# One excursion per pair of heads instead of two, with the values in the MLP's free banks

## The chip, the cores and the metric

The kernel runs on one core of one Trainium2 chip. The metric is the device time of one execution in microseconds (us), given as the median of several executions. The kernel before took 1018.84 us (four runs, 1018.21 to 1020.08). The engines are TensorE (PE in the profile; PEld is its weight load), VectorE (DVE), ScalarE (ACT), GpSimd (POOL) and SyncE (SP), which issues the DMAs here.

## The reference

A retention block feeds an MLP. There are 8 batches, 8 heads, 576 positions and 64 values per head, all in float32.

```python
scores = scale * np.matmul(q, k.transpose(0, 1, 3, 2))
Dmat = np.where(rel >= 0, gamma[:, None, None] ** rel[None, :, :], 0.0)
attn_out = np.matmul(scores * Dmat, v)              # per batch and head
x = attn_out.transpose(0, 2, 1, 3).reshape(B * S, H * D)   # 4608 x 512
h = x @ w_in                                        # 512 x 2048
g = np.maximum(h, 0.0) + alpha * np.minimum(h, 0.0)
out = g @ w_out                                     # 2048 x 512
```

## The kernel before

**Retention.** A head's 576 positions are cut into 9 chunks of 64. Because the decay is a power of the distance, everything before a chunk can be folded into a 64x64 running sum of k-times-v products. So a chunk needs three things: its own 64x64 scores, the running sum of the chunks before it, and the product of both with v and q (the "values"). Two heads are worked on together as a pair; there are 8 x 4 = 32 pairs, numbered n. For one pair TensorE does 18 score products (L614), 16 state products k-times-v (L620) and 18 value products (L656). In the trace each product shows as two MATMUL records.

**MLP.** The 4608 tokens are cut into 18 blocks of 256, numbered kb. The hidden width of 2048 is cut into 8 units, numbered i, and one unit is the work of `mlp_unit(kb, i)`: 14 products of x with w_in (L463, the tiles `ph`), a chain of 11 instructions on VectorE and one on ScalarE that forms `g` (L471 to L487), and 7 products of `g` with w_out (L381, the tiles `po`). It uses 7 products for 2x2 blocks instead of 8. The w_out products are put off by one unit (`pend`), so TensorE's order is ph(u), po(u-1), ph(u+1), po(u), and so on, where u counts units.

**PSUM banks.** There are eight. The MLP's `ph` has two (tags `psh0` and `psh1`, pool `ps_h`), its `po` has four (`ps_o`), and the retention has two (tag `psa`, pool `ps_a`), which take scores, states and values in turn.

**Three phases.** Batches 0 and 1 and the preparation of the weights are written in a fixed order by hand. From batch 2 on (about 160 us into the run, loop `for b in range(2, B)`) the tile framework's scheduler orders the instructions of each engine from the program below. It inserts the waits between engines. MLP units of the blocks that are ready stand in `queue`, and the four pairs of batch b are strewn among them, 16 or 24 units a batch. After the last batch 24 units remain with no retention among them.

**A pair in that loop.** At the unit `u` where the pair begins, `pair_front` puts the scores and states between ph(u) and po(u-1). The 18 score products do not fit with the states into two banks, so the two of the ninth chunk go into a free quarter of the unit's own bank, `ph[0][:, 3]`; the code calls it `extra`. VectorE multiplies the scores by mask and decay into `mt` (L625 for the ninth chunk, L636 for the rest), and ScalarE copies the queries beside them (L632). `running_sums` and `pair_sums` (L583 to L597) run after unit u+1. After unit u+2 come the scaling and transposing of the next pair (`scale_pair`, L528 and L533; `transposes`, L539) and `pair_values`: the 18 value products between po(u+1) and ph(u+3), which ScalarE copies into the tokens' tiles `xb` (L665). So TensorE leaves the MLP twice for each pair. The loads of the next pair's k, q and v are issued by SP (L97, L105) into buffers two deep; a v buffer comes free when the value products of the pair before last are done.

Of the kernel before, what the change touches and what calls it, by code (L numbers as in the profile page):

```python
# [18 lines left out]
def kernel(  # L19
# [49 lines left out]
    def half(x):  # L69
        return slice(x * C, (x + 1) * C)  # L70
# [377 lines left out]
                          (t[:, 2], b21, t[:, 1])):  # L448
            nc.gpsimd.tensor_tensor(out=o, in0=x0, in1=x1, op=ALU.subtract)  # L449

    def mlp_unit(kb, i, front=None):
        if kb not in xt:
            combine_x(kb)
        x, t = xb[kb], xt[kb]
        ph = [ps_h.tile([P, 4, P], FP32, tag=f"psh{m}", name=f"ph{m}_{kb}_{i}")
              for m in range(2)]

        for n, (m, o, l, r) in enumerate((
                (0, 2, 0, x[:, 0:2, 0:P]), (0, 0, 2, x[:, 2:4, 0:P]), (0, 1, 5, t[:, 1]),
                (1, 0, 4, t[:, 0]), (1, 1, 1, x[:, 0:2, P:TB]),  # L460
                (1, 2, 6, x[:, 2:4, P:TB]), (1, 3, 3, t[:, 2]))):
            for cc in range(2):
                nc.tensor.matmul(ph[m][:, o], w_in[i // UST][:, l, i % UST, cc], r[:, cc],  # L463
                                 start=(n in (0, 3) and cc == 0), stop=(n in (2, 6) and cc == 1),
                                 skip_group_check=True)

        rest = front(ph[0][:, 3]) if front else None


        g = mlp.tile([P, 8, P], FP32, tag="g", name=f"g_{kb}_{i}")  # L470
        nc.scalar.copy(g[:, 7], ph[0][:, 2])  # L471
        for o, x0, x1 in ((g[:, 0:5:4], ph[0][:, 0:2], g[:, 7:8].to_broadcast([P, 2, P])),
                          (g[:, 5:7], ph[1][:, 0:2], g[:, 4:5].to_broadcast([P, 2, P])),
                          (g[:, 3], ph[1][:, 0], g[:, 6]),
                          (g[:, 1:3], ph[1][:, 2:4], g[:, 5:7])):
            nc.vector.tensor_tensor(out=o, in0=x0, in1=x1, op=ALU.add)  # L476
        for m in range(2):
            fc = m * NU + i
            nc.vector.tensor_scalar(g[:, 4 + 2 * m:6 + 2 * m], g[:, 2 * m:2 * m + 2], 0.0,  # L479
                                    alpha[:, fc:fc + 1], ALU.min, ALU.mult)  # L480
        nc.vector.scalar_tensor_tensor(  # L481
            out=g[:, 0:4].rearrange("p x t -> p (x t)"),
            in0=g[:, 0:4].rearrange("p x t -> p (x t)"), scalar=0.0,
            in1=g[:, 4:8].rearrange("p x t -> p (x t)"), op0=ALU.max, op1=ALU.add)
        for o, x0, x1, op in ((4, 1, 3, ALU.add), (6, 0, 1, ALU.subtract),
                              (5, 4, 0, ALU.subtract), (7, 2, 5, ALU.subtract)):
            ins = nc.vector.tensor_tensor(out=g[:, o, :], in0=g[:, x0, :], in1=g[:, x1, :], op=op)  # L487

        combine(3, ins)
        assert i < NU - UST or not waiting  # L490
        if rest:
            rest()
        pend.append((kb, i, g))
        if len(pend) > 1:
            mlp_out()
# [11 lines left out]
            if ready[kb] == b:  # L507
                queue.extend((kb, i) for i in range(NU))

    def pop_units(n, front=None):  # L510
        for _ in range(min(n, len(queue))):
            kb, i = queue.pop(0)
            mlp_unit(kb, i, front)
            if i == NU // 2 and kb + 1 < NKB and ready[kb + 1] <= done[0]:
                combine_x(kb + 1)

# [4 lines left out]
    def ps_tile(shape, name):  # L521
        return ps_a.tile(shape, FP32, tag="psa", name=name)
# [19 lines left out]
    def chunk(j):  # L542
        return slice(j * C, (j + 1) * C)
# [51 lines left out]
    def pair_sums(vn, su):  # L595
        for h2 in range(2):
            nc.scalar.copy(vn[half(h2), h2, 1:], su[half(h2)])  # L597
# [2 lines left out]

    later = []

    def pair_front(n, kT, qT, kn, vn):
        c = pairs[n][1]
        mts[n] = mt = attn.tile([P, 2 * S], FP32, tag="at", name=f"mt_{n}").rearrange(
            "p (h j s) -> p h j s", h=2, s=C)
        assert C == D and NJ == 9

        def products(extra):
            ps = [ps_tile([P, 2, NM - 1, C], f"ps{p2}_{n}") for p2 in range(2)]  # L610
            for j in (NJ - 1, *range(NJ - 1)):
                for h2 in range(2):
                    x = half((1 - h2, h2)[j % 2])
                    nc.tensor.matmul(extra[x, 0:C] if j == NJ - 1 else ps[j % 2][x, 0, j // 2],  # L614
                                     kT[half(h2), chunk(j)], qT[half(h2), chunk(j)],
                                     start=True, stop=True, skip_group_check=True)
            for j in range(NJ - 1):
                for h2 in range(2):
                    x = half((h2, 1 - h2)[j % 2])
                    nc.tensor.matmul(ps[j % 2][x, 1, j // 2], kn[half(1 - h2), j],  # L620
                                     vn[half(1 - h2), h2, j], start=True, stop=True,
                                     skip_group_check=True)
            for h2 in range(2):
                to = half(1 - h2)
                nc.vector.scalar_tensor_tensor(  # L625
                    out=mt[to, h2, NJ - 1], in0=extra[to, 0:C],
                    scalar=th[to, 3, 2 * c + h2:2 * c + h2 + 1], in1=mask[to],
                    op0=ALU.mult, op1=ALU.mult)

            def rest():  # L630
                for h2 in range(2):
                    nc.scalar.copy(mt[half(h2), h2].rearrange("p j s -> p (j s)"), qT[half(h2)])  # L632
                for p2 in range(2):
                    for h2 in range(2):
                        h, to, x = 2 * c + h2, half(1 - h2), (1 - h2, h2)[p2]
                        nc.vector.scalar_tensor_tensor(  # L636
                            out=mt[to, h2, p2:NJ - 1:2], in0=ps[p2][half(x), 0],
                            scalar=th[to, 3, h:h + 1],
                            in1=mask[to, None, :].to_broadcast([C, NM - 1, C]),
                            op0=ALU.mult, op1=ALU.mult)  # L640
                later.append(lambda: pair_sums(vn, running_sums(n, ps[0][:, 1], ps[1][:, 1])))

            return rest

        return products

    def pair_values(n, vn, mt):
        b, c = pairs[n]
        w = TB // C

        j1 = -b * NJ % w or w
        j1 += w if NJ - j1 > 6 else 0
        pv = [ps_tile([P, (j1, NJ - j1)[i], C], f"pv{i}_{n}") for i in range(2)]
        for j in range(NJ):
            for h2 in range(2):
                nc.tensor.matmul(pv[j >= j1][half(h2), j - (j1 if j >= j1 else 0)],  # L656
                                 vn[:, h2, j], mt[:, h2, j], start=True, stop=True)
        j = 0
        while j < NJ:
            kb, o = divmod(b * NJ + j, w)  # L660
            if kb not in xb:
                xb[kb] = ring.tile([P, NCC, TB], FP32, tag=f"x{kb % NRING}", name=f"xb_{kb}")
            m, i = min(w - o, NJ - j), j >= j1
            j0 = j - (j1 if i else 0)
            nc.scalar.copy(xb[kb][:, c, o * C:(o + m) * C].rearrange("p (j s) -> p j s", s=C),  # L665
                           pv[i][:, j0:j0 + m])
            j += m
# [276 lines left out]
    enqueue(0)  # L944
    enqueue(1)

    for b in range(2, B):


        nq, first, at = len(queue), b * NPAIR, {}  # L950
        for c in range(NPAIR):
            u = c * nq // NPAIR
            while queue[u][1] in (0, NU - 1):
                u += 1
            assert u + 2 < nq and (not at or at[c - 1] + 2 < u)
            at[c] = u
        begin = {u: first + c for c, u in at.items()}
        for u in range(nq):
            front = None
            if u in begin:  # L960
                n = begin[u]
                if n + 1 < len(pairs) and n + 1 not in loaded:
                    loaded[n + 1] = load_pair(n + 1)
                front = pair_front(n, *turned.pop(n), loaded[n][0], loaded[n][3])
            pop_units(1, front)
            if u - 1 in begin:
                later.pop(0)()
            if u - 2 in begin:
                n = begin[u - 2]
                if n + 1 < len(pairs):  # L970
                    scale_pair(n + 1)
                    turned[n + 1] = transposes(n + 1)
                pair_values(n, loaded[n][3], mts.pop(n))
                del loaded[n]
        enqueue(b)
    pop_units(len(queue))
    while pend:
        mlp_out()
# [28 lines left out]
```

## Time and profile before

| | |
|---|---|
| median of four runs | 1018.84 us |
| the profiled execution's own time | 1019.2 us |
| its span, first to last instruction | 1017.5 us |
| TensorE busy | 1000.9 us (98%) |
| VectorE busy | 775.6 us (76%) |
| ScalarE busy | 269.8 us (27%) |
| GpSimd busy | 178.7 us (18%) |
| granted TensorE clock over the span | 0.995 |

The page lists busy time by engine, the chain of work that ended last, and groups of instructions by source line. A row of a group reads: line, engine, operation, output <- inputs, shape, count, then busy time and mean duration in ns, then the idle time of that engine just before and what ended it. A row of the timeline reads: start in us, length in us, engine, line, operation, output <- inputs, shape, count, and in square brackets an idle time before it with what ended that. Ends of matmuls are modelled, so distances between starts are used here for TensorE.

### The profile page before, as it was taken

The numbers are of one execution on the slowest core, as the hardware profiler recorded it, in microseconds if no ns is written. First come the engines' busy times: TensorE is split into PE (matmuls) and PEld (weight loads), VectorE is DVE, ScalarE is ACT, GpSimd is POOL, SyncE is SP. The second block draws the span as 40 slices with busy tenths as digits, with TensorE's granted clock in tenths as the row PEclk, the third lists the DMA queues.
The fourth block names the chain that finished last, engine by engine and source line by source line (L and its number), as shares of the span: only waits on it lengthen the run. The fifth ranks groups of instructions, "written<-read, shape, count | busy, mean of one in ns | idle before, by whom it ended". The sixth has DMA issues, their size and how long they took to land.

```text
span 1017.5 us, 23084 instructions
## 1 busy us (share of the span) xinstructions
PE 1000.9 (98%) x9385; PEld 894.1 (88%) x9385; DVE 775.6 (76%) x2086; ACT 269.8 (27%) x605; POOL 178.7 (18%) x201
## 2 busy tenths in 40 slices
PE   6999999999999999999999999999999999999997
PEld 5666668899999999999999999999999999999997
DVE  6769967878787888768778788887878777667665
ACT  4656652223222222122021312232222211000000
POOL 5656674300200020100010000200010001010000
PEclk8999999999999999999999999999999999999999
DMA  9975744322231313112112313222313000000000
GB/s 241 245 185 151 181 75 95 61 59 49 60 57 44 65 30 69 28 42 48 44 25 57 60 45 60 57 48 59 58 45 60 13 23 1 22 1 21 2 21 22
DMA packets 229307, 64.30 MB, mean 63 GB/s; under 512 B 214336, under 2 KB 222544, under 8 KB 229200
## 3 DMA queue, kind: packets, MB, share of 16 engines
q1 hardware_dynamic: 227088, 62.29, 26.9%
q8 instruction: 74, 1.21, 0.5%
q10 hardware_dynamic: 2112, 0.53, 0.3%
q14 instruction: 33, 0.27, 0.1%
HBM read 53.35 MB, written 9.44 MB: 62 GB/s over the span
## 4 chain that ended last, share of the span: by engine, by line
PE 95%; DVE 3%; DMA 1%; ACT 1%; issue 0%; SPq 0%; DVEq 0%; ACTq 0%
PE ph L463 38%; PE po L381 37%; PE ph L419 6%; PE po L398 6%; PE pv L656 3%; PE ps L614 1%; PE ps L620 1%; DMA w_out<-in_k_dram 1%; PE ph L614 1%; DVE su L589 0%; DVE g L476 0%; PE pt L697 0%; DVE mt L636 0%; PE pv L775 0%; PE ps L556 0%
## 5 line engine op out<-in xcount | busy, mean ns | idle before, releaser
L381 PE MATMUL po<-w_out,g 128*128 128x256 f32 x1792 | 411.0, 381 | 0.2
L381 PEld LDWEIGHTS po<-w_out,g 128*128 128x128 f32 x1792 | 330.2, 190 | 42.7 <-DVE g L487 1.4
L476 DVE TENSOR_TENSOR g<-ph,g 128x256 f32<-128x256 f32 (+1 forms) x512 | 186.6, 385 | 129.2 <-ACT g L471 77.1
L463 PE MATMUL ph<-xb,w_in 128*128 128x128 f32 x2048 | 272.7, 276 | 0.0
L463 PEld LDWEIGHTS ph<-xb,w_in 128*128 128x128 f32 x2048 | 257.1, 192 | 7.8 <-issue 0.7
L463 PE MATMUL ph<-xt,w_in 128*128 128x128 f32 x1536 | 213.8, 275 | 0.7 <-DVE g L476 0.7
L463 PEld LDWEIGHTS ph<-xt,w_in 128*128 128x128 f32 x1536 | 192.2, 192 | 1.0 <-PE ph L463 0.8
L487 DVE TENSOR_TENSOR g<-g 128x128 f32<-128x128 f32 x512 | 126.2, 287 | 5.4
L471 ACT COPY g<-ph 128x128 f32<-128x128 f32 x128 | 34.2, 267 | 328.3 <-PE ph L463 219.8
L528 POOL TENSOR_TENSOR qx<-qx,tabx 128x576 f32<-128x576 f32 x28 | 32.1, 1147 | 377.9 <-DVE g L476 256.8
L481 DVE SCALAR_TENSOR_TENSOR g<-g 128x512 f32<-128x512 f32 x128 | 91.3, 713 | 3.8
L479 DVE TENSOR_SCALAR g<-g,alpha 128x256 f32<-128x256 f32 x256 | 84.2, 370 | 2.9
L597 ACT COPY vn<-su 64x512 f32<-64x512 f32 x56 | 34.6, 618 | 134.0 <-DVE su L591 133.3
L419 PE MATMUL ph<-xb,w_in 128*128 128x256 f32 x256 | 61.5, 396 | 0.7 <-ACT xb L783 0.7
L398 PE MATMUL po<-w_out,g 128*128 128x512 f32 x128 | 58.6, 599 | 0.9 <-DVE g L435 0.9
L419 PEld LDWEIGHTS ph<-xb,w_in 128*128 128x128 f32 x256 | 49.9, 198 | 10.9 <-issue 2.4
L625 DVE SCALAR_TENSOR_TENSOR mt<-ph,th,mask 64x64 f32<-64x64 f32 x48 | 13.6, 283 | 53.2 <-PE ph L614 52.8
L665 ACT COPY xb<-pv 128x256 f32<-128x256 f32 (+3 forms) x84 | 22.7, 323 | 111.1 <-PE pv L656 111.0
L636 DVE SCALAR_TENSOR_TENSOR mt<-ps,th,mask 64x256 f32<-64x256 f32 x96 | 46.1, 480 | 2.4
L533 ACT ACTIVATE vn<-vn,tabv 64x576 f32<-64x576 f32 x56 | 43.4, 775 | 8.1 <-DMA vn<-in_v_dram 7.0
L398 PEld LDWEIGHTS po<-w_out,g 128*128 128x128 f32 x128 | 23.4, 190 | 24.5 <-issue 21.8
L449 POOL TENSOR_TENSOR xt<-xb 128x256 f32<-128x256 f32 x16 | 11.6, 727 | 188.5 <-PE ph L463 188.5
(134 smaller groups left out, 746.6 us busy)
## 6 DMA issues: line engine op xcount, KB each, us to landing
out_dram<-osb SPq DMA_DIRECT2D x36, 256.0 KB, 2.3
kx<-in_k_dram SPq DMA_DIRECT2D x112, 72.0 KB, 2.4
qx<-in_q_dram SPq DMA_DIRECT2D x112, 72.0 KB, 2.9
vn<-in_v_dram SPq DMA_DIRECT2D x56, 144.0 KB, 3.0
kn<-in_k_dram SPq DMA_DIRECT2D x56, 144.0 KB, 3.3
raw<-in_moe_w_in_dram SPq DMA_DIRECT2D x24, 256.0 KB, 4.0
raw<-in_moe_w_out_dram SPq DMA_DIRECT2D x10, 512.0 KB, 4.2
w_in<-in_moe_w_out_dram SPq DMA_DIRECT2D x6, 512.0 KB, 5.6
```

What stands on the lines that cost most here:

```text
L381: nc.tensor.matmul(acc[kb][n // 2][:, n % 2, :], g[:, x, :], w_out[i][:, y, :], start=(i == 0 and n % 2 == 0), stop=(i == NU - 1 and (n % ...
L398: nc.tensor.matmul(acc[kb][m], g[:, 2 * x + m], w_out[i][:, 2 * x:2 * x + 2].rearrange("p x f -> p (x f)"), start=(i == 0 and x == 0), sto ...
L419: nc.tensor.matmul(ph[:, x], w_in[i // UST][:, cc // 2 * 2 + x, i % UST, cc % 2], xb[kb][:, cc], start=(cc == 0 and x == 0), stop=(cc == N ...
L463: nc.tensor.matmul(ph[m][:, o], w_in[i // UST][:, l, i % UST, cc], r[:, cc], start=(n in (0, 3) and cc == 0), stop=(n in (2, 6) and cc == ...
L471: nc.scalar.copy(g[:, 7], ph[0][:, 2])
L476: nc.vector.tensor_tensor(out=o, in0=x0, in1=x1, op=ALU.add)
L479: nc.vector.tensor_scalar(g[:, 4 + 2 * m:6 + 2 * m], g[:, 2 * m:2 * m + 2], 0.0, alpha[:, fc:fc + 1], ALU.min, ALU.mult)
L481: nc.vector.scalar_tensor_tensor(out=g[:, 0:4].rearrange("p x t -> p (x t)"), in0=g[:, 0:4].rearrange("p x t -> p (x t)"), scalar=0.0, in1 ...
L487: ins = nc.vector.tensor_tensor(out=g[:, o, :], in0=g[:, x0, :], in1=g[:, x1, :], op=op)
L533: nc.scalar.activation(vn[x, h2], vn[x, h2], ACTF.Copy, scale=tabv[x, c:c + 1])
L597: nc.scalar.copy(vn[half(h2), h2, 1:], su[half(h2)])
L636: nc.vector.scalar_tensor_tensor(out=mt[to, h2, p2:NJ - 1:2], in0=ps[p2][half(x), 0], scalar=th[to, 3, h:h + 1], in1=mask[to, None, :].to_ ...
```

## The change

The value products of pair n-1 and the scores and states of pair n are now issued together, in a function `joint(n)`, between two MLP units: after po(u-1) and before ph(u+1). For the values it takes the two banks of the MLP, `psh0` and `psh1`, which unit u has left and unit u+1 will take. The ninth chunk's scores (`extra`) go into the last eighth of the second of these banks, beside the values there. The running sums follow after the next unit, and scaling and transposing of the next pair after the one behind it. There are 25 such excursions (the first has no values, the last no front) where there were 48.

```diff
-    def mlp_unit(kb, i, front=None):
+    def mlp_unit(kb, i):
...
-        rest = front(ph[0][:, 3]) if front else None
...
-        if rest:
-            rest()
...
-    def pair_front(n, kT, qT, kn, vn):
+    def pair_front(n, kT, qT, kn, vn, extra):
...
-                    nc.tensor.matmul(extra[x, 0:C] if j == NJ - 1 else ps[j % 2][x, 0, j // 2],
+                nc.tensor.matmul(extra[x] if j == NJ - 1 else ps[j % 2][x, 0, j // 2],
...
-    def pair_values(n, vn, mt):
+    def pair_values(n, vn, mt, pv=None):
...
-        pv = [ps_tile([P, (j1, NJ - j1)[i], C], f"pv{i}_{n}") for i in range(2)]
+        pv = pv or [ps_tile([P, (j1, NJ - j1)[i], C], f"pv{i}_{n}") for i in range(2)]
...
+    def operands(n):
+        scale_pair(n)
+        turned[n] = transposes(n)
+
+    def joint(n):
+        pv = [ps_h.tile([P, 8, C], FP32, tag=f"psh{m}", name=f"pv{m}_{n}") for m in range(2)]
+        if n - 1 in mts:
+            pair_values(n - 1, loaded.pop(n - 1)[3], mts.pop(n - 1), pv)
+        if n == len(pairs):
+            return
+
+        pair_front(n, *turned.pop(n), loaded[n][0], loaded[n][3], pv[1][:, 7])
+        if n + 1 < len(pairs):
+            if n + 1 not in loaded:
+                loaded[n + 1] = load_pair(n + 1)
+            later.append(lambda: operands(n + 1))
+
+    mts.clear()
+    n = 2 * NPAIR
     for b in range(2, B):
-        nq, first, at = len(queue), b * NPAIR, {}
-        for c in range(NPAIR):
-            u = c * nq // NPAIR
-            while queue[u][1] in (0, NU - 1):
-                u += 1
...
-            pop_units(1, front)
-            if u - 1 in begin:
-                later.pop(0)()
-            if u - 2 in begin:
-                n = begin[u - 2]
-                if n + 1 < len(pairs):
-                    scale_pair(n + 1)
-                    turned[n + 1] = transposes(n + 1)
-                pair_values(n, loaded[n][3], mts.pop(n))
-                del loaded[n]
+        nq = len(queue)
+        at = [u + (u % NU == 0) for u in (c * nq // NPAIR + 2 for c in range(NPAIR))]
+        if b == 2:
+            at = [0, 3] + at[1:]
+        for u in range(nq):
+            first = queue[0][1] == 0
+            pop_units(1)
+            if later and not first:
+                later.pop(0)()
+            if u in at:
+                assert not later
+                joint(n)
+                n += 1
         enqueue(b)
```

The multiplications by mask and decay, the copies and the sums are the same instructions as before, on the same engines.

More of the change, by code (lines that the diff above doesn't have):

```diff
@@ L508, in enqueue, with pop_units @@
                 queue.extend((kb, i) for i in range(NU))
-    def pop_units(n, front=None):
+    def pop_units(n):
         for _ in range(min(n, len(queue))):
             kb, i = queue.pop(0)
-            mlp_unit(kb, i, front)
+            mlp_unit(kb, i)
             if i == NU // 2 and kb + 1 < NKB and ready[kb + 1] <= done[0]:
@@ L607, in pair_front @@
         assert C == D and NJ == 9
[L609 to L622, printed above, removed]
-            for h2 in range(2):
-                to = half(1 - h2)
+        ps = [ps_tile([P, 2, NM - 1, C], f"ps{p2}_{n}") for p2 in range(2)]
@@ new lines, in pair_front @@
+        for j in (NJ - 1, *range(NJ - 1)):
+            for h2 in range(2):
+                x = half((1 - h2, h2)[j % 2])
+                nc.tensor.matmul(extra[x] if j == NJ - 1 else ps[j % 2][x, 0, j // 2],
+                                 kT[half(h2), chunk(j)], qT[half(h2), chunk(j)],
+                                 start=True, stop=True, skip_group_check=True)
+        for j in range(NJ - 1):
+            for h2 in range(2):
+                x = half((h2, 1 - h2)[j % 2])
+                nc.tensor.matmul(ps[j % 2][x, 1, j // 2], kn[half(1 - h2), j],
+                                 vn[half(1 - h2), h2, j], start=True, stop=True,
+                                 skip_group_check=True)
@@ new lines, in pair_front @@
+        for h2 in range(2):
+            nc.scalar.copy(mt[half(h2), h2].rearrange("p j s -> p (j s)"), qT[half(h2)])
+        for h2 in range(2):
+            to = half(1 - h2)
+            nc.vector.scalar_tensor_tensor(
+                out=mt[to, h2, NJ - 1], in0=extra[to],
+                scalar=th[to, 3, 2 * c + h2:2 * c + h2 + 1], in1=mask[to],
+                op0=ALU.mult, op1=ALU.mult)
+        for p2 in range(2):
+            for h2 in range(2):
+                h, to, x = 2 * c + h2, half(1 - h2), (1 - h2, h2)[p2]
@@ L625, in products @@
                 nc.vector.scalar_tensor_tensor(
-                    out=mt[to, h2, NJ - 1], in0=extra[to, 0:C],
-                    scalar=th[to, 3, 2 * c + h2:2 * c + h2 + 1], in1=mask[to],
+                    out=mt[to, h2, p2:NJ - 1:2], in0=ps[p2][half(x), 0],
+                    scalar=th[to, 3, h:h + 1],
+                    in1=mask[to, None, :].to_broadcast([C, NM - 1, C]),
                     op0=ALU.mult, op1=ALU.mult)
[L630 to L641, printed above, removed]
@@ L643, in products @@
-            return rest
-        return products
-    def pair_values(n, vn, mt):
+        later.append(lambda: pair_sums(vn, running_sums(n, ps[0][:, 1], ps[1][:, 1])))
+    def pair_values(n, vn, mt, pv=None):
         b, c = pairs[n]
@@ L945 @@
     enqueue(1)
-    for b in range(2, B):
-        nq, first, at = len(queue), b * NPAIR, {}
-        for c in range(NPAIR):
-            u = c * nq // NPAIR
-            while queue[u][1] in (0, NU - 1):
-                u += 1
-            assert u + 2 < nq and (not at or at[c - 1] + 2 < u)
-            at[c] = u
-        begin = {u: first + c for c, u in at.items()}
-        for u in range(nq):
[L959 to L964, printed above, removed]
-            pop_units(1, front)
-            if u - 1 in begin:
-                later.pop(0)()
-            if u - 2 in begin:
-                n = begin[u - 2]
-                if n + 1 < len(pairs):
-                    scale_pair(n + 1)
-                    turned[n + 1] = transposes(n + 1)
-                pair_values(n, loaded[n][3], mts.pop(n))
-                del loaded[n]
+    def operands(n):
[14 more added lines that the diff above has]
+    n = 2 * NPAIR
+    for b in range(2, B):
+        nq = len(queue)
+        at = [u + (u % NU == 0) for u in (c * nq // NPAIR + 2 for c in range(NPAIR))]
+        if b == 2:
+            at = [0, 3] + at[1:]
+        for u in range(nq):
+            first = queue[0][1] == 0
+            pop_units(1)
+            if later and not first:
+                later.pop(0)()
+            if u in at:
+                assert not later
+                joint(n)
+                n += 1
         enqueue(b)
+    assert n == len(pairs) + 1
     pop_units(len(queue))
```

## The prediction

> **What bounds the kernel now.** I read the busy shares and the chain first.
>
> ```profile
> PE 1000.9 (98%) x9385; PEld 894.1 (88%) x9385; DVE 775.6 (76%) x2086; ACT 269.8 (27%) x605; POOL 178.7 (18%) x201
> PE 95%; DVE 3%; DMA 1%; ACT 1%; issue 0%; SPq 0%; DVEq 0%; ACTq 0%
> ```
>
> TensorE is busy 98% of the span and holds 95% of the chain that ended last, so only what changes TensorE's own sequence counts. Next, TensorE's timeline around one excursion for values and one for scores and states.
>
> ```profile
> 510.06 3.19 PE L381 MATMUL po<-w_out,g 128*128 128x256 f32 x14
> 513.18 1.27 PE L656 MATMUL pv<-mt,vn 128*64 128x64 f32 x36
> 514.38 1.16 PE L463 MATMUL ph<-xb,w_in 128*128 128x128 f32 x8
> ...
> 517.60 3.19 PE L381 MATMUL po<-w_out,g 128*128 128x256 f32 x14
> ...
> 523.75 3.19 PE L381 MATMUL po<-w_out,g 128*128 128x256 f32 x14
> 526.78 1.05 PE L463 MATMUL ph<-xb,w_in 128*128 128x128 f32 x8
> ...
> 529.90 3.19 PE L381 MATMUL po<-w_out,g 128*128 128x256 f32 x14
> ...
> 539.07 1.05 PE L463 MATMUL ph<-xb,w_in 128*128 128x128 f32 x8
> ...
> 542.29 0.27 PE L614 MATMUL ph<-qT,kT 64*64 64x64 f32 x2
> ...
> 542.87 0.68 PE L620 MATMUL ps<-vn,kn 64*64 64x64 f32 x31
> 543.49 3.29 PE L381 MATMUL po<-w_out,g 128*128 128x256 f32 x14
> 546.61 1.05 PE L463 MATMUL ph<-xb,w_in 128*128 128x128 f32 x8
> ```
>
> A unit with nothing in between goes from po to the next po in 529.90 - 523.75 = 6.15 us (3.03 for po, 3.12 for ph). With the values it takes 517.60 - 510.06 = 7.54, so that excursion costs 1.39. From ph to the next ph with scores and states it is 546.61 - 539.07 = 7.54, again 1.39. A pair costs 2.78 us, and TensorE waits in neither.
>
> Then ScalarE's timeline after value products of three pairs, which begin at 257.18, 513.18 and 580.23 us on TensorE. These rows carry the forecast.
>
> ```profile
> 258.14 0.77 ACT L665 COPY xb<-pv 128x128 f32<-128x128 f32 x3 [4.73 <-PE pv L656]
> 514.49 0.49 ACT L665 COPY xb<-pv 128x256 f32<-128x256 f32 x2 [0.21 <-PE pv L656]
> 581.55 0.54 ACT L665 COPY xb<-pv 128x256 f32<-128x256 f32 x2 [0.38 <-PE pv L656]
> ```
>
> The last copy ends 1.73, 1.80 and 1.86 us after the first value product (258.91 - 257.18, and so on). Nobody waits for it on TensorE now: the next ph goes to other banks.
>
> **The change part by part.** *Two excursions become one.* Within the values 18 products start over 1.27 - 0.22 = 1.05 us, and the next ph follows 0.15 after the last start; 0.10 more is lost before them (3.12 for po instead of 3.03) and 0.10 in the ph after them. For scores and states 34 products start over 1.04 us (542.29 to 542.87 + 0.68 - 0.22 = 543.33), then 0.16, with 0.10 lost on either side. A joint without any wait would take 0.10 + 1.05 + 0.15 + 1.04 + 0.15 + 0.10 = 2.59, which saves 0.19. The 0.15 between values and scores is the nearest row's: early in the run products on 64x64 tiles go over to 64x32 tiles with 0.15 between starts (38.65 to 38.80) where 0.01 to 0.06 is usual. The Trainium skill, page "TensorEngine Tiling (Array Packing)", section "Tiling Modes", has the rule: changing the tiling mode drains TensorE. By that rule three changes of mode replace four, so it speaks for the change; by a free change between values and scores a joint without a wait would be 0.15 cheaper still, while one with the wait below costs the same either way, because the wait is longer.
>
> *The new wait.* `extra` lies in the second value bank. In the built order of TensorE's instructions the scores of this bank come after 6, 6, 7, 7, 9 or 10 other score products, depending on the batch (mean 7.5), and their first one waits for ScalarE's last copy out of that bank. The MLP shows the same kind of ordering today:
>
> ```profile
> ACT g L471 <- DVE mt L625: 107.5, 24, 8.6
> ```
>
> ScalarE's copy reads the third quarter of `ph[0]` and VectorE's L625 the fourth, and yet the copy waits in all 24 pairs. The Trainium skill says on the page "PSUM — Partial Sum Buffer", section "PSUM bank collisions raise a hardware error", that semaphores must guard PSUM by bank and quadrant, not by address. That rule speaks against the change: with it the wait stands and the joints cost +4.1 us in all, as worked out next; without it they would save 23 x 0.19 = 4.4 us.
>
> Counted from the first value product, the 7.5 scores are out at 1.05 + 0.15 + 7.5 x 0.03 = about 1.45. The number and size of the copies go by the batch, and their end does too: 1.73 for the pairs of batches 2 and 6, 1.80 for batch 4, 1.86 for batch 5 as above, and 1.69 for batches 3 and 7 (values from 311.94, three copies from 312.79 over 0.84). Over 23 joints (three of batch 7, four of each other) the mean is 1.75. Then 26.5 products are left. At 1.04/34 = 0.031 each, restart within, they take 0.82. So the joint costs 0.10 + 1.75 + 0.05 + 0.82 + 0.15 + 0.10 = 2.97, or 0.19 more than 2.78. The 0.05 from the copy's end to the matmul is a row on 64 partitions at 40.90 us (copy ends 40.85). Bounds: with the 26.5 at the bare pace of 0.029 and no restart, +0.10; with 0.14 for the release, as at 19.21 us after a copy that ended at 19.07, +0.28. I take 0.18, since the 0.05 row has the same tile height. Times 23 joints that hold both parts: +4.1 us, with ends +2.3 and +6.4. The first and the last excursion hold one part each, as before: nothing.
>
> *What is queued behind.* During the wait nothing else of TensorE can pass, and that is counted. ScalarE: L632 (two of 0.67) follows the copies and ends at 3.1. VectorE: its unit is over at about 0.9, L625 waits for `extra` and ends at 2.7, the transposing of the next queries (0.77, waits for L632) at 3.9, the four of L636 at 5.8. Then ScalarE's sum copy L583 and one scaling of v (0.78) stand ahead of L471 of unit u+1, which ends at 6.3. The first read of its ph is over at 6.7, the last at 8.8. ph(u+2) starts at 2.8 + 6.2 = 9.0 and needs the second bank 1.3 later: 1.5 us of cover. g is through L481 at 10.8, po(u+1) starts at 12.1: 1.3 us of cover. I cost this at nothing; without that cover each us late would be 23 us. The v reload behind the value products on SP lands as now (L533 began 4.25 after them), before ScalarE comes to it at 5.2; q and k reloads move with their transposes, and GpSimd's order is the same, with the scaling L528 ahead of need.
>
> *Stalls that can go.* Where GpSimd's weight sums slow VectorE's sums, TensorE waits today:
>
> ```profile
> 171.40 1.84 DVE L589 SCALAR_TENSOR_TENSOR su<-su,gch 128x64 f32<-128x64 f32 x2
> 175.26 0.68 PE L463 MATMUL ph<-xt,w_in 128*128 128x128 f32 x4 [0.68 <-DVE g L476]
> ```
>
> Counting starts against 3.12 and 3.03, ph at 173.08 and 195.57 and the po after each lose 0.92 + 0.26 + 0.35 + 0.35, and two later po 0.07 and 0.14: 2.1 us in all. The sums now run a unit after the scores, with the cover above, and the slowing was about 1.6 us in a unit (1.84 for two of L589 where 1.01 is usual, 1.09 for the third where 0.28 is). I take 1.5 us as gone; ends: 0 and 2.1. What is late next there is the same sum chain, 0.1 to 0.2 us over its cover.
>
> *Sum.* +4.1 - 1.5 = +2.6 us on the profiled execution's 1019.2 (span 1017.5), so 1021.8; that execution is 0.36 above the median of the four runs, so the median goes from 1018.84 to about 1021.4.
>
> **The rivals.** *The wait is hidden* (the other side). If `extra` is reached after the copies are over, or does not wait, each joint saves 0.19 instead: -4.4 - 1.5, so 1012.9 us. It decides when the copies end before about 1.45 us. Against it: they end at 1.69 at the earliest in the rows above, with ScalarE idle before them. Chance 0.07.
>
> *Nothing to measure.* The restart is at the cheap end (+2.3) and all 2.1 of stalls go, or any mix that ends within 2.0 us of 1018.84: 1017 to 1020.9. For it: each size is only 0.1 us a pair. Chance 0.23.
>
> *VectorE becomes the bound.* Between two joints of a 16-unit batch lie 4 units: TensorE 4 x 6.15 + 2.97 = 27.6 us, VectorE 4 x 4.1 for units, 5.5 for the pair, 1.5 for its share of the output sums, 23.4, and some 1.7 idle around L625. For it: the pair's work now falls into one unit more closely. Against it: 1.3 us of cover at the tightest place. If it is over by 0.3 us in each, +6.9: 1028. Chance 0.08.
>
> *The forecast*, a wait of about 0.3 us in every joint: 0.62, with its own range of 1020.9 to 1025.
>
> **How the numbers follow.** A difference of about 0.2% (2 us) is what a measurement of this kernel can tell from no change. Slower is the forecast and VectorE's case, 0.62 + 0.08 = 0.70; within 0.2% is 0.23; faster is the hidden wait, 0.07. The range leaves out about 0.07 for the hidden wait and part of the tail of VectorE's case: the low end is +2.3 - 2.1 - about 0.4 for the runs' spread, 1018.6; the high end +6.4 with no stall gone and a little of VectorE's case, 1026.0.
>
> **What would show it.** In the profile after: L645 (the values), then a run of L609, then an idle of 0.2 to 0.4 us of the weight loads before `pv` L609 put down to ACT `xb` L654, 23 times; po to the next po over a joint 6.15 + 2.97 = 9.1 us; ph and po of the other units at 3.12 and 3.03; no wait of ph or po for VectorE longer than now. I am wrong if that wait is missing (then faster), if VectorE ends waits of TensorE in every joint (then far slower), or if the joint is 2.8 or less.

## The result, and the profile after

The kernel after takes 1021.41 us (median of 36 runs, 1018.85 to 1026.52). The kernel before, run beside it, takes 1019.21 us (56 runs). The ratio is 1.0019, with a 95% interval of 1.0013 to 1.0025. By the ratio it is slower by 1.9 us (the two medians lie 2.2 apart), and that is at the bound of 0.2% that the prediction gave for what a measurement can tell. The profiled execution took 1021.06 us with a span of 1019.3 us, where before it was 1019.2 and 1017.5.

Busy shares and the chain by engine, from the page of the kernel after:

```profile
PE 999.5 (98%) x9385; PEld 894.2 (88%) x9385; DVE 771.2 (76%) x2086; ACT 269.8 (26%) x605; POOL 178.6 (18%) x201
PE 95%; ACT 2%; DVE 1%; issue 1%; POOL 0%; DVEq 0%; ACTq 0%
```

ScalarE rises from 1% of the chain to 2%, and VectorE falls from 3% to 1%. TensorE's busy time fell by 1.4 us (its ends are modelled), and yet the run is longer. The waits of TensorE's weight loads between 160 and 860 us of the kernel after say which wait is new (the columns are the total in us, how often, and the longest):

```profile
PEld pv L645 <- DVE g L485: 7.6, 23, 0.3
PEld pv L609 <- ACT xb L654: 6.3, 23, 0.5
PEld pv L645 <- issue: 0.3, 1, 0.3
```

and the first three rows of the same view of the kernel before, where the value products are L656:

```profile
PEld pv L656 <- issue: 8.0, 24, 0.3
PEld po L381 <- DVE g L487: 1.4, 4, 0.5
PEld ph L463 <- PE ph L463: 0.8, 1, 0.8
```

The wait at L645 is the old one at L656: 0.33 us of the weight loads ahead of each set of value products, in both kernels, and the products themselves start on time. The second row is new: `extra` waits for ScalarE's copies of the values 23 times, once in each joint that holds both parts. The waits of po and ph for VectorE are gone. One joint in the timeline of the kernel after:

```profile
178.99 1.27 PE L645 MATMUL pv<-mt,vn 128*64 128x64 f32 x36
...
179.96 0.77 ACT L654 COPY xb<-pv 128x128 f32<-128x128 f32 x3 [5.40 <-PE pv L645]
...
180.19 0.45 PE L609 MATMUL ps<-qT,kT 64*64 64x64 f32 x12
...
180.78 0.14 PEld L609 LDWEIGHTS pv<-qT,kT 64*64 64x64 f32 x2 [0.28 <-ACT xb L654]
180.78 0.27 PE L609 MATMUL pv<-qT,kT 64*64 64x64 f32 x2
...
180.90 0.46 PE L609 MATMUL ps<-qT,kT 64*64 64x64 f32 x18
...
181.18 0.65 PE L615 MATMUL ps<-vn,kn 64*64 64x64 f32 x32
...
181.75 1.16 PE L463 MATMUL ph<-xb,w_in 128*128 128x128 f32 x8
```

Six score products (12 records) go to the retention's own banks. Then TensorE stands until the third copy is over at 179.96 + 0.77 = 180.73, and `extra` starts 0.05 later.

The joints differ among themselves, and that is a test without any edit. In 20 of the 23 the length goes with the end of the last copy, counted from the first value product: 1.69 us gives a joint of 2.91, 1.73 to 1.74 gives 2.96, 1.80 gives 3.02 and 1.86 gives 2.97. (At 1.86 ten other scores are out before the wait, at 1.80 nine, so the joint is a little shorter.) Three stand apart with later copies or fewer scores ahead, at 393.10 (3.07), 552.78 (3.02, copies over at 1.91) and 663.07 us (3.20, copies over at 1.97). The mean over all is 2.974 us, where the two excursions before cost 1.390 + 1.396 = 2.786.

**The sum of it.** The load-bound opening ends at a slightly different time in each execution: the first ph of the last phase starts at 152.83 us before, at 152.50 after, and between 151.2 and 155.3 in the experiments below. So single profiled executions are compared here by what follows that start, to the end of the span:

| kernel | first ph | span behind it | against before | mean joint |
|---|---|---|---|---|
| before | 152.83 | 864.62 | | (2.786 in two) |
| after | 152.50 | 866.85 | +2.2 | 2.974 |
| `extra` in the first value bank | 152.24 | 862.71 | -1.9 | 2.761 |
| `extra` last | 155.29 | 858.07 | -6.6 | 2.591 |
| before, values in the MLP's banks | 153.38 | 865.98 | +1.4 | |
| before, without the last weight sums | 151.22 | 862.79 | -1.8 | |
| after, two sums once more | 152.27 | 866.84 | +2.2 | 2.961 |
| after, two sums twice more | 153.11 | 874.15 | +9.5 | 2.962 |

After against before: 23 x (2.974 - 2.786) = +4.3 for the joints and -2.1 for the stalls that vanished, in all +2.2.

### The profile page after: what moved, and what is told of

Same layout as the page of the kernel before. It is cut to its first block, busy times and chain, and to the rows that moved or that the text cites. A ratio compares the mean times of both kernels' runs of the same rounds, so it can differ in the third digit from the quotient of the medians.

```text
span 1019.3 us, 23122 instructions
## 1 busy us (share of the span) xinstructions
PE 999.5 (98%) x9385; PEld 894.2 (88%) x9385; DVE 771.2 (76%) x2086; ACT 269.8 (26%) x605; POOL 178.6 (18%) x201
## 4 chain that ended last, share of the span: by engine, by line
PE 95%; ACT 2%; DVE 1%; issue 1%; POOL 0%; DVEq 0%; ACTq 0%
PE ph L463 40%; PE po L381 38%; PE po L398 6%; PE ph L419 5%; PE pv L645 3%; ACT xb L654 2%; PE ps L615 1%; PE pv L609 1%; PE ps L609 1%; PE ps L552 0%; PE pu L725 0%; PE pu L570 0%; ACT wa L296 0%; PE ps L705 0%; DVE gch L240 0%
## 5 line engine op out<-in xcount | busy, mean ns | idle before, releaser
L524 POOL TENSOR_TENSOR qx<-qx,tabx 128x576 f32<-128x576 f32 x28 | 32.6, 1163 | 355.2 <-DMA qx<-in_q_dram 291.2
L479 DVE SCALAR_TENSOR_TENSOR g<-g 128x512 f32<-128x512 f32 x128 | 89.8, 701 | 3.0
L477 DVE TENSOR_SCALAR g<-g,alpha 128x256 f32<-128x256 f32 x256 | 84.9, 374 | 3.7
L419 PE MATMUL ph<-xb,w_in 128*128 128x256 f32 x256 | 58.9, 383 | 2.7 <-ACT xb L772 1.5
L449 POOL TENSOR_TENSOR xt<-xb,xt 128x256 f32<-128x256 f32 x32 | 23.4, 732 | 111.1 <-ACT xb L654 110.4
```

Source lines behind the costliest of these rows:

```text
L419: nc.tensor.matmul(ph[:, x], w_in[i // UST][:, cc // 2 * 2 + x, i % UST, cc % 2], xb[kb][:, cc], start=(cc == 0 and x == 0), stop=(cc == N ...
L479: nc.vector.scalar_tensor_tensor(out=g[:, 0:4].rearrange("p x t -> p (x t)"), in0=g[:, 0:4].rearrange("p x t -> p (x t)"), scalar=0.0, in1 ...
```

## The experiments

The theory was the forecast's: a joint saves one change of mode (0.19 us), but `extra` waits for ScalarE, and the stalls that GpSimd caused go. The rival was that the wait for `extra` is not what costs, and that the joint is dear by itself or by what it does to VectorE's order. Each ratio is to the kernel before as run beside that experiment (median 1019.81 us up to the first try on the stalls, 1019.63 for the rest).

**Where `extra` lies.** The first edit puts the ninth chunk's scores into the first value bank, whose copies are over earlier:

```diff
-        pair_front(n, *turned.pop(n), loaded[n][0], loaded[n][3], pv[1][:, 7])
+        pair_front(n, *turned.pop(n), loaded[n][0], loaded[n][3], pv[0][:, 7])
```

> The changed kernel with one word altered: the ninth chunk's scores go into the last eighth of the first value bank instead of the second. Theory (TensorE waits for ScalarE's last copy out of the bank that these scores share): the copies out of the first bank end 1.51, 1.34, 1.10 and 0.94 us after the first value product (batches 2 and 6, 3 and 7, 4, 5), and the built order now puts 3, 1, 0 and 0 scores ahead. So the wait shrinks to about 0.3 and 0.15 us and is gone in batches 4 and 5: a joint costs about 2.87, 2.76, 2.6 and 2.6 us by batch instead of 2.96, 2.91, 3.02 and 2.97. Over 23 joints that is 5 us less than the changed kernel: about 1016.4 us, 2.5 to 3 us below the kernel before. The next ph waits for VectorE's L622 in this version; it should be over in time. Rival (the lost time belongs to putting values and scores side by side, whatever the bank): no change against the changed kernel, 1021 us, with a gap of 0.3 us in every joint of batches 4 and 5 too.

Measured: 1017.51 us, ratio to before 0.9977 (0.9967 to 0.9988). The joints take 2.91 (batches 2 and 6), 2.78 (3 and 7) and 2.59 (4 and 5). In batch 4 one large copy clears the first bank, and the timeline of this kernel shows how it ends before anybody needs it:

```profile
392.76 1.27 PE L645 MATMUL pv<-mt,vn 128*64 128x64 f32 x36
...
393.55 0.37 ACT L654 COPY xb<-pv 128x256 f32<-128x256 f32 x1 [5.22 <-PE pv L645]
...
393.98 0.27 PE L609 MATMUL pv<-qT,kT 64*64 64x64 f32 x2
...
394.13 0.49 ACT L654 COPY xb<-pv 128x256 f32<-128x256 f32 x2 [0.21 <-PE pv L645]
```

The first copy ends at 393.92; `extra` starts at 393.98 as the first of the scores, 0.17 us after the last value product's start. In the seven other joints of batches 4 and 5 it is 0.15, the change of tile mode, so at most 0.02 us of it is a wait. The other two copies run until 394.62 and hold nobody up. So the price goes with the copy that frees `extra`'s bank, and not with the joint. In the very first excursion, which has no values, ph now waits 0.6 us for VectorE to read `extra` out of its first bank, which was expected to be over in time. The joints and the stalls that went make -2.7; this wait is most of what separates the table's -1.9 from it.

**When `extra` comes.** The second edit keeps the bank and takes the two score products of the ninth chunk to the end of the joint, behind the other 16 scores and the 16 states:

```diff
-        for j in (NJ - 1, *range(NJ - 1)):
+        def score(j):
...
+            score(j)
+        for j in range(NJ - 1):
...
+        score(NJ - 1)
```

> The changed kernel with the ninth chunk's scores issued last, after the other 16 scores and the 16 states, still in the second value bank. Theory (the wait for ScalarE's copy): the products ahead of them last until about 2.2 us after the first value product, the copies are over at 1.69 to 1.86, so no wait is left. A joint costs about 2.6 us instead of 2.96: 23 x 0.36 = 8.3 us less than the changed kernel, 1013 us, 0.6% below the kernel before, and what is left of the gain is one change of mode per pair, 0.19 us, and the 2 us of stalls that had gone already. Rival (the gap is the price of the second change of mode or of writing beside values that are being read): the gap stays where the scores begin or moves with the ninth chunk, 1021 us. Second rival (VectorE comes too late with the ninth chunk's product, so the next ph waits): a wait of the next ph for VectorE in each joint, 1015 to 1021 us.

Measured: 1012.65 us, ratio 0.9931 (0.9919 to 0.9944). It is faster than both kernels, by 0.7% against before. Every joint takes 2.591 us. TensorE's timeline of one of them in this kernel:

```profile
393.11 1.27 PE L648 MATMUL pv<-mt,vn 128*64 128x64 f32 x36
394.31 0.69 PE L609 MATMUL ps<-qT,kT 64*64 64x64 f32 x32
394.82 0.65 PE L617 MATMUL ps<-vn,kn 64*64 64x64 f32 x32
395.29 0.28 PE L609 MATMUL pv<-qT,kT 64*64 64x64 f32 x4
395.50 1.16 PE L463 MATMUL ph<-xb,w_in 128*128 128x128 f32 x8
```

`extra` starts at 395.29, 2.18 us after the first value product, and the last copy was over at 394.97, 1.86 us after it. There is no gap but the 0.15 us at the change from values to scores. This is the joint without any wait that the prediction put at 2.59, and it saves 2.786 - 2.591 = 0.195 us per pair. The wait in the kernel after thus cost 23 x (2.974 - 2.591) = 8.8 us, twice what the joint saves.

**Only the values' banks.** The third edit makes one part of the change alone: two excursions as before, but the values go to the MLP's banks:

```diff
-        pv = [ps_tile([P, (j1, NJ - j1)[i], C], f"pv{i}_{n}") for i in range(2)]
+        pv = ([ps_h.tile([P, 8, C], FP32, tag=f"psh{i}", name=f"pv{i}_{n}") for i in range(2)]
+              if b >= 2 else [ps_tile([P, (j1, NJ - j1)[i], C], f"pv{i}_{n}") for i in range(2)])
```

> The kernel before with one part of the change alone: two excursions as before, but the values of batches 2 to 7 go into the MLP's two banks. Theory: a bank that ScalarE still copies from holds up TensorE, so the next ph, due 1.20 us after the first value product, waits for the copies out of the first bank, which end at 1.51 or 1.34 in batches 2, 3, 6 and 7 and before 1.20 in batches 4 and 5. With 0.1 for the release that is 0.4 or 0.25 us in 16 of 24 pairs, +5 us against the kernel before (1024 us); the scheduler has moved one product of the next po or of the scores in front of the ph in some pairs, which may hide or add up to 0.3 us each, so +1 to +8. Rival (the banks cost nothing, only the shared bank of the ninth chunk does): 1019.2 us, no wait of ph for ScalarE.

Measured: 1020.63 us, ratio 1.0009 (1.0001 to 1.0018), at the low end of what was expected. The waits of TensorE's weight loads for ScalarE in this kernel (160 to 880 us) come to little:

```profile
PEld ph L463 <- ACT xb L666: 0.6, 4, 0.2
```

The scheduler had put other work between the values and ph. In TensorE's timeline of this kernel the values are followed by three score products of the next pair here:

```profile
669.40 1.27 PE L657 MATMUL pv<-mt,vn 128*64 128x64 f32 x36
670.60 0.34 PE L614 MATMUL ps<-qT,kT 64*64 64x64 f32 x6
670.96 1.16 PE L463 MATMUL ph<-xb,w_in 128*128 128x128 f32 x8
```

In seven other pairs one or three scores go between, and in eight a w_out product. The wait I meant to measure is mostly covered, and the eight pairs whose scores are split pay one change of tile mode more. Each of them takes about 0.25 us longer for it, 2.0 us in all; 0.7 us of the stalls are gone here too, and the two come near the +1.4 of the table without any wait for ScalarE. So this run does not show what a ph behind the values would pay for the copies.

**The stalls that went.** The prediction laid the stalls of the kernel before to GpSimd's weight sums (L324). The first try to take these away missed:

```diff
+    waiting.clear()
     ordered.close()
```

> The kernel before, with the sums of the last weight blocks that GpSimd makes during the first units of the third phase left out (so the products with these weights use what lies there). Theory (the stalls near 173 and 196 us come from GpSimd slowing VectorE's running sums): they go, 1.9 us less than before, 1017.3 us. Rival (the chain of running sums stands too close behind the scores whatever GpSimd does): the stalls stay, 1019.2 us.

Measured: 1019.74 us, ratio 1.0003 (0.9994 to 1.0012), ph still held for 0.92 and 0.28 us. But the trace shows the L324 sums at 170 to 195 us as before: a later call adds them to the list again. This run says nothing on the cause. The next edit leaves the sums out where they are listed:

```diff
-            waiting.extend((w_in[i // UST], x) for x in S_WORK)
-            waiting.extend((w_out[j], x) for j in range(i + 1 - UST, i + 1) for x in T_WORK)
+            if i < NU - 1:
+                waiting.extend((w_in[i // UST], x) for x in S_WORK)
+                waiting.extend((w_out[j], x) for j in range(i + 1 - UST, i + 1) for x in T_WORK)
+            else:
+                for w in (w_in[i // UST], w_out[i - 1], w_out[i]):
+                    nc.gpsimd.memset(w[:, 4:7], 0.01)
```

> The kernel before, with the weight sums of the last two blocks of weights left out: their sum slots are set to a constant as soon as the last pieces are unpacked, so GpSimd has no L324 left between 165 and 200 us (part of what the kernel computes is left out). My account of the stalls in the kernel before (ph at 173.08 and 195.57 us, and the po after each, 1.9 us together, laid to GpSimd's weight sums slowing VectorE's score sums beside them): the slowed sums go back from about 0.9 to about 0.5 us each and the 1.9 us go, so about 0.2% faster than before and no wait of ph over 0.1 us in that stretch. Rival: the stalls come from the order of VectorE's work alone, and stay at 0.9 and 0.3 us for ph, with the time as before.

Measured: 1017.16 us, ratio 0.9977 (0.9968 to 0.9986), so 1.4 to 3.3 us faster. VectorE's groups by shape between 160 and 200 us show the slowed instructions, first in the kernel before, then in this one (four lines lower):

```profile
L589 DVE SCALAR_TENSOR_TENSOR su<-su,gch 128x64 f32<-128x64 f32 x6 | 5.1, 856 | 0.1
L585 DVE SCALAR_TENSOR_TENSOR su<-su,gch,ps 64x256 f32<-64x256 f32 x4 | 1.9, 478 | 0.1
```

```profile
L593 DVE SCALAR_TENSOR_TENSOR su<-su,gch 128x64 f32<-128x64 f32 x6 | 2.0, 340 | 0.1
L589 DVE SCALAR_TENSOR_TENSOR su<-su,gch,ps 64x256 f32<-64x256 f32 x4 | 1.9, 478 | 0.1
```

The six instructions on `su` and `gch` alone, which lie in SBUF, fall from 856 to 340 ns on average. The four that also read `ps`, in PSUM, are unchanged, though two of them (at 170.88 and 193.37 us) ran beside L324 too. How the six were slowed stands in VectorE's and GpSimd's timelines of the kernel before, near the second stall:

```profile
193.89 1.43 DVE L589 SCALAR_TENSOR_TENSOR su<-su,gch 128x64 f32<-128x64 f32 x2
...
195.57 0.85 DVE L589 SCALAR_TENSOR_TENSOR su<-su,gch 128x64 f32<-128x64 f32 x1
```

```profile
193.03 2.21 POOL L324 TENSOR_TENSOR w_out<-w_out 128x256 f32<-128x256 f32 x3 [5.57 <-DVE g L487]
195.20 1.15 POOL L528 TENSOR_TENSOR qx<-qx,tabx 128x576 f32<-128x576 f32 x1
```

The sums end at 195.32 and 196.42 us, each about 0.08 after a GpSimd instruction (195.24 and 196.35 us). All six end so: five beside L324, the last beside the scaling L528 that stood in line behind it. They are not stretched by a factor, they are held until GpSimd's instruction is over. No unit of ph in this stretch is held any more, where two were, by 0.92 and 0.26. The span behind the first ph is 1.8 us shorter, as expected. The theory holds: the stalls were GpSimd's sums beside VectorE's. The 0.5 us that I expected of each slowed sum was too high. In the kernel after, the sums of L324 still run in this stretch, but beside other work of VectorE: they hold two L477, at 172.07 and 173.35 us, for 1.35 and 1.43 us where 0.35 is usual. The sum L585 at 186.48 us takes 0.95 beside the scaling L524. All of this falls where there is cover.

**The cover on VectorE.** The prediction costed what is queued behind the wait at nothing, with 1.5 us of cover for the second bank of ph(u+2) and 1.3 us for po(u+1). In the trace after it is 1.46 us and 1.60 us in most joints; the least is 0.86 and 1.00 in the first and 1.08 and 1.22 in the second, where GpSimd holds one sum for 0.7 us. To see whether this is real, VectorE gets more to do behind each joint: the first two score sums (L581) are repeated, once or twice, with the same result:

```diff
-        for h2 in range(2):
+        for h2 in (0, 1) * (2 if n >= 2 * NPAIR else 1):
```

> The kernel after, with VectorE's first two score sums of each pair done once more in the blocks with joint excursions (same values, 0.97 us more of VectorE in the unit behind each of 23 joints). The cover that I costed at nothing was 1.46 us for the second bank of ph(u+2) and 1.60 us for po(u+1) in the changed kernel: by that it shrinks to about 0.5 and TensorE loses nothing: the same time as after, 1021 to 1022, joints still 2.98. Rival (VectorE is nearly the bound already): TensorE waits for VectorE in a unit behind each joint, 0.3 us or more each, 1028 or above.

Measured: 1022.26 us, ratio to before 1.0024 (1.0013 to 1.0035), where after has 1.0019: no difference. The covers shrink to 0.71 and 0.98 us in most joints. Only the unit behind the joint at 800.55 us loses something, 0.3 us. The joints take 2.96.

With `(3 if ...)` in the same place, two more repetitions:

> As the run with one repetition, but with two (1.94 us more of VectorE behind each joint). By the measured cover of 1.5 us TensorE now waits for VectorE by 0 to 0.5 us behind each joint, 1021 to 1033. Rival (nothing of VectorE's sums is near TensorE's path): no change against after. If the cover was wrongly read and there is none, 23 times 1.9 us, 1065.

Measured: 1028.51 us, ratio 1.0083 (1.0065 to 1.0101). Two rows of the waits of TensorE's weight loads in this kernel (160 to 880 us), and the place where one wait ends in its timeline:

```profile
PEld po L381 <- DVE g L479: 6.2, 13, 0.9
PEld pv L609 <- ACT xb L654: 6.0, 23, 0.3
```

```profile
238.51 1.15 POOL L524 TENSOR_TENSOR qx<-qx,tabx 128x576 f32<-128x576 f32 x1 [11.93 <-DMA qx<-in_q_dram]
238.61 1.45 DVE L477 TENSOR_SCALAR g<-g,alpha 128x256 f32<-128x256 f32 x2
...
240.60 0.69 DVE L479 SCALAR_TENSOR_TENSOR g<-g 128x512 f32<-128x512 f32 x1
241.21 0.28 DVE L585 SCALAR_TENSOR_TENSOR su<-su,gch 128x64 f32<-128x64 f32 x1
...
241.35 3.29 PE L381 MATMUL po<-w_out,g 128*128 128x256 f32 x14 [0.50 <-DVE g L479]
```

Now po(u+1) waits for g, just the row to which the prediction counted the smaller cover. The span behind the first ph grows by 7.3 us against after, which is 0.32 us for each of 23 joints on average. By the measured cover of 1.60 us, 1.94 us of extra work leave 0.34. That this agrees is luck, for the loss is not even: behind 15 of the joints TensorE loses 0.17 to 0.93 us, behind the other 8 at most 0.06. In each of the 15 GpSimd's scaling L524 now falls beside an L477 of the same unit and holds it for 0.12 to 0.88 us, as at 238.61 above (1.45 us for two of L477, where 0.61 is usual). Behind the six joints where GpSimd holds nothing TensorE loses nothing, and in five of them g's L479 is over 0.24 to 0.38 us before po(u+1) starts. So VectorE is off the path in the kernel after, with somewhat more to spare behind a joint than the 1.60 us that were read. The 7.3 us come from the extra work and GpSimd's holds together, not from the extra work alone.

## Why the prediction was right

*The new wait.* Foretold: a joint of 2.97 us, +4.1 us in all (the terms give 0.19 over 2.78, and 0.18 was taken). Measured: 2.974 us, +0.188, +4.3. The ends of the copies, read from a kernel in which nobody on TensorE waited for them, came out within 0.01 us (1.69, 1.73, 1.80, 1.86) in 18 of the 23 joints, and so did the release of 0.05 us in all. The prediction read one or two pairs of a batch, and missed that the first pair is later: by 0.05 us in batches 3, 4, 5 and 7, as in the trace before already (1.74 at 290.71 us, for example), and by 0.24 once, at 663.07 us. The mean end is 1.77 and not 1.75 us. That the joint came out right to 0.01 is thus partly luck, for what follows the wait is 0.02 us shorter than the 0.97 foretold. The upper bound of 0.14 us for the release was not needed. The two runs that move `extra` show that this wait, and not the joint, makes the change slow.

*The saving.* Foretold 0.19 us per pair, measured 0.195 in the joints without a wait. The 0.15 us between values and scores, taken from 64x32 tiles early in the run, is 0.15 in every joint. Of the Trainium skill's rule that a change of tiling mode drains TensorE ("TensorEngine Tiling (Array Packing)", "Tiling Modes"), the runs show the price here: one excursion fewer, and so three changes in place of four, is worth 0.195 us a pair. Its rule that PSUM is guarded by bank and quadrant, not by address ("PSUM — Partial Sum Buffer", "PSUM bank collisions raise a hardware error"), fits as well: `extra` and the values share no address, and moving `extra` to the other bank moved the wait to that bank's copies. These are waits that the tile framework puts in; what the chip would do without them no run here shows.

*The stalls that can go.* This term was mis-sized: I took 1.5 of 2.1 us as gone, and all 2.1 went. I expected a rest of 0.1 to 0.2 us where the sum chain is late against its cover; the cover behind a joint is longer than I feared, and nothing is late. A reading was off too: the row of 1.01 us for two sums that the prediction called usual (551.08 us) was itself held by GpSimd's scaling L528, which ran from 550.54 to 551.69. Two sums alone take 0.60 (at 169.78 us in the run without the last weight sums), so the slowing in that unit was 2.0 us and not 1.6. The cause I named is shown for the four early stalls (1.9 us); the two small later ones of po were not tested.

*The cover.* Costed at nothing, and nothing it was, in every joint. The sizes were 1.46 for 1.5 and 1.60 for 1.3 in most joints, and 0.86 and 1.00 at the least.

*The sum.* +4.3 - 2.1 = +2.2 us in place of +4.1 - 1.5 = +2.6. With more runs, the median of before rose by 0.4 us to 1019.21. These two small differences cancel in the predicted time: 1021.4 against 1021.41. So close an agreement is partly luck. "Slower by over 0.2%" was given 0.70, and the measured 0.19%, with an interval to both sides of the bound, is neither clearly that nor "within".

*The rivals.* The hidden wait needed copies that end before 1.45 us; none did, and the run with `extra` last shows what it would have been worth: 1012.65 us, where the rival said 1012.9. VectorE as the bound was foretold at 1028 if it were over by 0.3 us per joint; the run with two repetitions loses 0.32 on average, by way of GpSimd's holds, and takes 1028.51. "Nothing to measure" comes nearest to being true beside the forecast, by way of all stalls going.

## What to carry to other kernels

When work moves into a buffer that another engine still empties, read when that engine ends from the trace of before, count from the same start when the first user arrives, and put the user that shares the buffer last: here two of 34 products in another place turned +0.2% into -0.7%. A saving of a fraction of a microsecond on the engine that bounds is worth having only if no new wait stands in it, so look at each product's bank by itself. A stall that a second engine causes by holding up a third can vanish merely because the held work lands where there is cover, and come back when more work puts the hold on the path, as in the run with two repetitions.

## What the runs showed of the hardware

TensorE's restart after a copy out of the bank is very even: `extra` starts 0.05 us after ScalarE's last copy in all 23 joints, whatever the batch. And GpSimd holds some of VectorE's instructions up until its own is over. In the third phase of the kernel before, all 27 of VectorE's sums on `su` and `gch` that began with more than 0.2 us of a GpSimd instruction still to run end 0.08 us after it, however long that was; alone they take 0.28. It goes by the operands, at the same operation and shape too: of VectorE's TENSOR_TENSOR of 128x128, the four `g<-g` that began beside GpSimd took 0.70 to 0.82 us instead of 0.28, and the fifteen `g<-ph,g`, which read `ph` in PSUM, kept their 0.28 to 0.29. So did the other instructions with an operand in PSUM, such as the 64x256 sums with 478 ns. But the transposes L539, from SBUF to SBUF, are not held either (0.73 to 0.77 us), so lying in SBUF is not the whole condition, and no run here shows what it is.
